# The first row block of a layer norm, DFT and MLP kernel: rows only centered, the factor of each row multiplied onto the hidden units, loads issued by two engines

## The chip, the cores and the metric

The kernel runs on one core of one Trainium2 chip. The metric is the device time of one execution in microseconds (us). Lower is better.

## The reference

For an input x of S = 2048 rows and D = 640 columns the reference computes, cut to what matters:

```python
xn = (x - mean(x)) / sqrt(var(x) + 1e-5)          # by row
a  = einsum("bsd,ed->bse", xn, dft_hid_re)
b  = einsum("bsd,ed->bse", xn, dft_hid_im)
y  = einsum("ts,bse->bte", dft_seq_re, a) - einsum("ts,bse->bte", dft_seq_im, b)
h  = gelu(einsum("bsd,df->bsf", xn, w1) + b1, approximate=True)     # F = 1536 hidden units
out = x + y + einsum("bsf,fd->bsd", h, w2) + b2
```

The change is in the first quarter of the rows of the MLP (the line of h and the last product). What matters for it: the mean is taken off a row ahead of the product with w1, and the factor 1/sqrt(var + 1e-5) is one number for each row, so that it can be multiplied in ahead of the product or behind it, as long as it is ahead of b1 and gelu.

## The kernel before

**Numbers.** TensorE multiplies operands of a type called fp32r. Every fp32 operand is split into a high part (a copy of type fp32r) and a low part (the rest), and a product is three matmuls: high by high, high by low, low by high. `split` (L154 to L161) does this: ScalarE (ACT) copies the high part at L160, VectorE (DVE) subtracts at L161. So each operand costs one instruction on ACT and then one on DVE.

**Tiling.** The MLP works with rows as the free axis of its products: the 2048 rows are cut in 4 blocks of 512, the 640 columns in ND = 5 tiles of 128, the 1536 hidden units in NF = 12 groups of 128, called units here. For a block of rows, `hidden(g)` (L289 to L304) makes unit g: 5 column tiles by 3 matmuls = 15 products of 128x512, summed in PSUM bank g % 3. `gelu(g)` (L310 to L320) takes the bank: gelu with the bias b1 on ACT (L314, into the tile `ab`), the high part on ACT (L318), the low part on DVE (L320), both into `hs`. `output(g)` (L322 to L333, with `product` at L277 to L279) makes 15 products with w2 into banks 3 to 7, where the five output tiles of a block stay until its 12 units are through. `outs` then clears the banks: bias on ACT (L344), transpose on DVE (L347), addition to x on GpSimd (POOL, L349). Block 0 is units g = 0 to 11, block 1 is g = 12 to 23. Behind these two blocks come the DFT and the rest of the MLP, which the change does not touch.

**The order.** The schedule is manual: each engine executes its instructions in the order in which the program writes them and waits where an operand isn't there yet. DMAs are issued by SyncE (SP) nearly everywhere, in written order too. So the order of calls is the order in each queue.

**The start.** `load_x` (L178) loads the first 512 rows as four chunks of 128 rows, all issued on SP. While they travel, 19 warm-up matmuls on zeros (L648) keep TensorE (PE) at work; they read tiles that share buffers with the raw w1 tiles, so the loads of w1 (L255) wait until the warm-up is through with these. For each chunk DVE takes mean and variance (`ln_stats`, L185 and L186; for chunk 1 ACT does it by two sums, L672 to L678), then `ln_scale` (L192 to L197) makes the factor: a root on ACT, a reciprocal and one Newton step on DVE. The rows are centered and multiplied (chunks 0 and 1 on ACT, L686; chunks 2 and 3 on DVE, L208), PE transposes them (`transpose_x`, L667) into banks 3 to 7, and `split` brings the five banks to SBUF as `xtt`, the operand of the units. The first piece of w1 is split at L706 and L711. Then come `hidden(0)` and `hidden(1)`, with the preparation of w1 and w2 for the next units between.

**The loop over units.** From there a loop runs over g. For each unit i of block 0 it writes, in this order:

```python
prep_w1(i + 3); prep_w2(i + 1)      # splits of w1 and w2: ACT, DVE
load_w1(i + 6); load_w2(i + 4)      # SP
first_block(i)
acc = hidden(g + 2)                 # PE
gelu(g + 2, acc)                    # ACT, ACT, DVE
output(g)                           # PE
```

`first_block(i)` (L886 to L912) prepares the later blocks beside this. At i = 0 and 1 the normed rows 0 to 3 (chunks) are made again and stored to a DRAM tile `xs`. At i = 2 to 5 DVE takes the statistics of chunks 4 to 7. At i = 6 their factor and scaling (L201) follow, then 16 stores to `xs` (L203) and four loads of `z`, which brings block 1's rows back in the order in which DVE can transpose them. At i = 8 and 9 DVE does the first two transposes of z (`transpose_z`, L238) and the statistics of chunks 8 to 11. In the iteration i = 9 the five splits of block 1's `xtt` stand between `hidden(11)` and `gelu(11)`. At i = 10 chunks 8 to 11 are scaled and stored, and at i = 11 the matrices of the hidden DFT begin to be loaded (`wraw`) and are transposed on DVE (L372) and split in the units of block 1. The last two iterations of block 0 have another order on PE: output(10), hidden(12), hidden(13), output(11).

Of the kernel before, what the change touches and what calls it, by code (L numbers as in the profile page):

```python
# [15 lines left out]
P = 128  # L16
Q = 4
B = 32
EPS = 1e-5
NWARM = 19  # L20
NGATE = (7, 10)
TAIL = 4
PADL = 8


@with_exitstack
def kernel(
# [78 lines left out]
    def bank(k):  # L106
        return banks[:, k]
# [68 lines left out]
    def load_x(c, eng=nc.sync):  # L176
        xt[c] = row_tile(f"x{c}")
        eng.dma_start(xt[c], x[c * P : (c + 1) * P])  # L178

    def ln_stats(c):  # L180
        m = MV
        st = ST[c % 2]
        half = D // 2
        for h in range(2):
            nc.vector.bn_stats(st[:, h, :], xt[c][:, h * half : (h + 1) * half])  # L185
        nc.vector.bn_aggr(m[:, c % 4, 0:2], st.rearrange("p a b -> p (a b)"))  # L186

    def ln_scale(c0, n):

        m = MV[:, c0 % 4 : c0 % 4 + n]  # L190
        ve, r, t = m[:, :, 2], m[:, :, 3], m[:, :, 4]
        nc.scalar.activation(r, m[:, :, 1], AF.Sqrt, bias=eps[:, 0:1])  # L192
        nc.vector.tensor_scalar(ve, m[:, :, 1], EPS, None, op0=ALU.add)
# [11 lines left out]
    def ln_apply_chunked(dst, c, j0=0, j1=ND):  # L205

        m = MV[:, c % 4]
        nc.vector.tensor_scalar(  # L208
            chunked(dst)[:, :, j0:j1],
            xt[c].rearrange("p (q c i) -> p q c i", q=Q, i=B)[:, :, j0:j1],  # L210
            m[:, 0:1],
            m[:, 3:4],
            op0=ALU.subtract,
            op1=ALU.mult,
        )
# [29 lines left out]

    W1, W2, w1r, w2r = {}, {}, {}, {}

    def load_w1(i, eng=nc.sync):
# [5 lines left out]
        for q in range(Q):  # L254
            eng.dma_start(t[q * B : (q + 1) * B], v[q, :, :, i * P : (i + 1) * P])  # L255

    def load_w2(i, eng=nc.sync):
        if i >= NF:
# [27 lines left out]
    def unit(g):  # L286
        return g if g < NF else LATE[g % NF]

    def hidden(g):  # L289
        i = unit(g)  # L290
        acc = bank(g % 3)
        kinds = ((0, 0), (0, 1), (1, 0))
        steps = [(j, k) for j in range(ND) for k in range(3)]
        if g == 0:
            steps = FIRST
        if g == 1:

            steps.sort(key=lambda s: s[1] == 2)
        for n, (j, k) in enumerate(steps):
            a, b = kinds[k]  # L300
            nc.tensor.matmul(  # L301
                acc, W1[i][:, a, j * P : (j + 1) * P], XT[j][:, b], start=n == 0, stop=n == len(steps) - 1
            )
        return acc  # L304
# [5 lines left out]
    def gelu(g, acc, fill=lambda k: None):  # L310

        i = unit(g)
        a = AB[:, g % 2]
        nc.scalar.activation(a, acc, AF.Gelu_apprx_tanh, bias=b1c[:, i : i + 1])  # L314
        fill(0)
        hs = HS[:, g % 3]
        HT[g] = hs
        nc.scalar.activation(hs[:, 0], a, AF.Copy)  # L318
        fill(1)
        nc.vector.tensor_tensor(hs[:, 1], a, hs[:, 0].bitcast(F32), op=ALU.subtract)  # L320

    def output(g):  # L322
        t, i = divmod(g, NF)
        if i == 0:
            oacc[t] = [bank(3 + e) for e in range(ND)]
        second(t, i, unit(g), HT[g])
# [301 lines left out]

    zeros = rows.tile([P, TB], F32, tag="yt", bufs=2, name="zeros")

    warms = [early.tile([P, TB], F32R, tag="w1r", bufs=3, name=f"warm{k}") for k in range(3)]
# [6 lines left out]
    for warm in warms:  # L638
        nc.vector.tensor_copy(warm, zeros)

    nc.scalar.activation(eps[:, 1:2], eps[:, 0:1], AF.Sqrt)
    load_w1(0)
    load_w1(1)

    wacc = bank(0)
    for k in range(NWARM):
        warm = warms[sum(k >= n for n in NGATE)]
        nc.tensor.matmul(wacc, warm[:, :P], warm, start=True, stop=True)  # L648
    load_w1(2)
    load_w2(0)  # L650
# [1 line left out]
    load_w2(1)  # L652
    load_w2(2)

    for tag, size, keys in PLACES:
        t = whole[tag] = place(tag, (P, size // 4))
        for k, key in enumerate(keys):
            slots[key] = t[:, k * 2 * D : (k + 1) * 2 * D].rearrange("p (a b) -> p a b", a=2)
    for j in range(ND):
        new_xt(0, j)  # L660
    tacc = [bank(3 + j) for j in range(ND)]
# [5 lines left out]
            nc.tensor.transpose(tacc[j][:, c * P : (c + 1) * P], xp[:, c, j * P : (j + 1) * P], ident)  # L667


    m = MV[:, 1]  # L670
    scratch = AB.rearrange("p a b -> p (a b)")
    nc.scalar.activation(scratch[:, :D], xt[1], AF.Copy, accum_out=m[:, 4:5])  # L672
    ln_stats(0)
    ln_scale(0, 1)
    nc.scalar.activation(m[:, 5:6], m[:, 4:5], AF.Copy, scale=-1.0 / D)
    nc.scalar.activation(scratch[:, :D], xt[1], AF.Square, bias=m[:, 5:6], accum_out=m[:, 2:3])
    nc.scalar.activation(m[:, 1:2], m[:, 2:3], AF.Copy, scale=1.0 / D)
    nc.scalar.activation(m[:, 0:1], m[:, 5:6], AF.Copy, scale=-1.0)  # L678

    def center(c):  # L680
        n = MV[:, c]
        nc.vector.scalar_tensor_tensor(n[:, 5:6], n[:, 0:1], -1.0, n[:, 3:4], op0=ALU.mult, op1=ALU.mult)

    def apply_on_act(c, j0, j1):
        n = MV[:, c]
        nc.scalar.activation(  # L686
            chunked(xp[:, c])[:, :, j0:j1],
            xt[c].rearrange("p (q c i) -> p q c i", q=Q, i=B)[:, :, j0:j1],
            AF.Identity,
            bias=n[:, 5:6],  # L690
            scale=n[:, 3:4],
        )

    center(0)
    apply_on_act(0, 0, ND)
    for c in (2, 3):
        ln_stats(c)
    transpose_x(0, 0, ND)
    ln_scale(1, 3)
    center(1)  # L700

    W1[0], first_w1 = slots[1, 0], w1r.pop(0).rearrange("p a b -> p (a b)")
    for j0, j1 in ((0, 2), (2, ND)):
        apply_on_act(1, j0, j1)
        if j0 == 0:
            nc.scalar.activation(W1[0][:, 0], first_w1, AF.Copy)  # L706
        for c in (2, 3, 1):
            if c != 1:
                ln_apply_chunked(xp[:, c], c, j0, j1)
            transpose_x(c, j0, j1)  # L710
    nc.vector.tensor_tensor(W1[0][:, 1], first_w1, W1[0][:, 0].bitcast(F32), op=ALU.subtract)  # L711
# [6 lines left out]
    acc0 = hidden(0)  # L718
    prep_w1(1)
    acc1 = hidden(1)  # L720
    prep_w2(0)
    prep_w1(2)
    load_w2(3)
    load_w1(5)

# [277 lines left out]
    for g in range(NG):  # L1003
        t, i = divmod(g, NF)
        if t == 0:
            prep_w1(i + 3)
            prep_w2(i + 1)
            load_w1(i + 6)
            load_w2(i + 4)
            first_block(i)  # L1010
            if i == NF - 1:
                open_w()
                acc = hidden(g + 2)
                output(g)

                def fill(k):
                    for e in ((0,), (1, 2))[k]:
                        add_block(xo[0], e, oacc[0][e], f"ot0_{e}", bias=b2c[:, e : e + 1])

                gelu(g + 2, acc, fill)  # L1020
                outs(0, (3, 4))
            elif i == NF - 2:
                output(g)
                gelu(g + 2, hidden(g + 2))
            else:
                acc = hidden(g + 2)
# [703 lines left out]
```

## Time and profile before

| | us |
|---|---|
| three runs before | 853.48, 853.95, 853.95 |
| their median | 853.95 |
| the profiled execution, its own time | 853.7 |
| its span on the core | 851.9 |
| PE busy | 842.7 (99%) |
| DVE busy | 661.1 (78%) |
| ACT busy | 353.6 (42%) |
| POOL busy | 48.1 (6%) |
| mean clock granted to TensorE | 0.998 |

In the rows of the timeline the first number is the start from the beginning of the span, the second the time that the group covers, both in us; then come the engine, the source line, the operation, what it writes and reads, the shapes, the count, and in brackets the idle time ahead of the group with what ended it. SPq is SyncE's queue of DMA issues. The time of a group of matmuls ends with the last one's drain, so that one matmul of 128x512 alone reads 0.39 us, though in a row of them one follows another every 0.23. Durations of rows that follow each other on one engine overlap a little for the same reason.

### The profile page before, as it was taken

The numbers are of one execution on the slowest core, as the hardware profiler recorded it, in microseconds if no ns is written. First come the engines' busy times: TensorE is split into PE (matmuls) and PEld (weight loads), VectorE is DVE, ScalarE is ACT, GpSimd is POOL, SyncE is SP. The second block draws the span as 40 slices with busy tenths as digits, with TensorE's granted clock in tenths as the row PEclk, the third lists the DMA queues.
The fourth block names the chain that finished last, engine by engine and source line by source line (L and its number), as shares of the span: only waits on it lengthen the run. The fifth ranks groups of instructions, "written<-read, shape, count | busy, mean of one in ns | idle before, by whom it ended". The sixth has DMA issues, their size and how long they took to land.

```text
span 851.9 us, 10326 instructions
## 1 busy us (share of the span) xinstructions
PE 842.7 (99%) x3711; PEld 695.8 (82%) x3711; DVE 661.1 (78%) x836; ACT 353.6 (42%) x496; POOL 48.1 (6%) x69
## 2 busy tenths in 40 slices
PE   8999999999999999999999999999999999999997
PEld 6888888878888888888888888888888888888885
DVE  7554766785758888879979787889967998885686
ACT  7443634456666554343444343232323423222241
POOL 0000211031211300000000000000000000000001
PEclk9999999999999999999999999999999999999999
DMA  7757698937669998958744679663865779704464
GB/s 186 215 143 199 142 228 233 225 81 190 206 223 349 360 208 161 185 110 200 160 137 105 168 215 293 159 145 97 208 169 169 252 191 228 303 19 179 125 179 99
DMA packets 207235, 158.45 MB, mean 186 GB/s; under 512 B 80848, under 2 KB 180688, under 8 KB 206672
## 3 DMA queue, kind: packets, MB, share of 16 engines
q1 hardware_dynamic: 198880, 136.03, 62.6%
q0 software_dynamic: 4080, 20.97, 6.2%
q10 hardware_dynamic: 4224, 0.79, 0.4%
q8 instruction: 29, 0.48, 0.2%
q14 instruction: 22, 0.18, 0.1%
HBM read 114.76 MB, written 42.99 MB: 185 GB/s over the span
## 4 chain that ended last, share of the span: by engine, by line
PE 98%; DVE 1%; DMA 0%; ACT 0%; issue 0%; SPq 0%; ACTq 0%
PE banks L277 29%; PE banks L279 29%; PE banks L278 29%; PE banks L301 10%; DMA x<-in_A_x_dram 0%; PE banks L667 0%; DVE st L185 0%; ACT ab L672 0%; DVE yo L1695 0%; ACT mv L192 0%; DVE mv L186 0%; DVE xp L208 0%; SPq L178 0%; DVE mv L194 0%; DVE mv L196 0%
## 5 line engine op out<-in xcount | busy, mean ns | idle before, releaser
L277 PE MATMUL banks<-as,xab 128*128 128x512 f32 x411 | 159.9, 389 | 0.0
L279 PE MATMUL banks<-as,xab 128*128 128x512 f32 x411 | 159.9, 389 | 0.0
L278 PE MATMUL banks<-as,xab 128*128 128x512 f32 x411 | 159.9, 389 | 0.0
L160 ACT ACTIVATE as<-r 128x1024 fp32r<-128x1024 f32 x80 | 85.0, 1062 | 177.0 <-PE banks L279 149.2
L161 DVE TENSOR_TENSOR as<-r,as 128x1024 fp32r<-128x1024 f32 x80 | 97.2, 1216 | 41.7 <-ACT as L160 41.6
L278 PEld LDWEIGHTS banks<-as,xab 128*128 128x128 f32 x411 | 77.1, 188 | 16.1
L277 PEld LDWEIGHTS banks<-as,xab 128*128 128x128 f32 x411 | 77.1, 188 | 16.1
L279 PEld LDWEIGHTS banks<-as,xab 128*128 128x128 f32 x411 | 77.1, 188 | 16.0
L277 PE MATMUL banks<-as,xc 128*128 128x512 f32 x224 | 87.1, 389 | 0.0
L278 PE MATMUL banks<-as,xc 128*128 128x512 f32 x224 | 87.1, 389 | 0.0
L279 PE MATMUL banks<-as,xc 128*128 128x512 f32 x224 | 87.1, 389 | 0.0
L160 ACT ACTIVATE as<-rt 128x1024 fp32r<-128x1024 f32 x32 | 34.0, 1063 | 70.8 <-PE banks L279 62.8
L301 PE MATMUL banks<-xtt,xab 128*128 128x512 f32 x240 | 56.9, 390 | 0.0
L301 PEld LDWEIGHTS banks<-xtt,xab 128*128 128x128 f32 x240 | 45.0, 188 | 9.7 <-ACT xtt L160 0.5
L278 PEld LDWEIGHTS banks<-as,xc 128*128 128x128 f32 x224 | 42.0, 188 | 8.8
L279 PEld LDWEIGHTS banks<-as,xc 128*128 128x128 f32 x224 | 42.0, 188 | 8.8
L277 PEld LDWEIGHTS banks<-as,xc 128*128 128x128 f32 x224 | 42.0, 188 | 8.7
L161 DVE TENSOR_TENSOR as<-rt,as 128x1024 fp32r<-128x1024 f32 x32 | 38.8, 1212 | 5.3 <-ACT as L160 5.3
L320 DVE TENSOR_TENSOR hs<-ab,hs 128x512 fp32r<-128x512 f32 x24 | 17.6, 733 | 32.2 <-ACT hs L318 32.2
L160 ACT ACTIVATE as<-u 128x1024 fp32r<-128x1024 f32 (+1 forms) x24 | 22.1, 919 | 48.2 <-PE banks L279 48.2
L488 DVE STREAM_TRANSPOSE r<-raw 128x1024 f32<-128x1024 f32 x32 | 39.5, 1240 | 2.3 <-PE banks L279 1.8
L488 DVE STREAM_TRANSPOSE rt<-raw 128x1024 f32<-128x1024 f32 x32 | 38.8, 1230 | 0.9 <-PE banks L279 0.8
(336 smaller groups left out, 1618.2 us busy)
## 6 DMA issues: line engine op xcount, KB each, us to landing
raw<-in_A_dft_seq_re_dram SPq DMA_DIRECT2D x64, 256.0 KB, 5.8
raw<-in_A_dft_seq_im_dram SPq DMA_DIRECT2D x64, 256.0 KB, 5.1
ws<-wit SPq DMA_DIRECT2D x15, 384.0 KB, 4.1
x<-in_A_x_dram SPq DMA_DIRECT2D x16, 320.0 KB, 4.1
xs<-x SPq DMA_DIRECT2D x64, 80.0 KB, 1.8
xo<-in_A_x_dram SPq DMA_DIRECT2D x16, 320.0 KB, 6.4
xab<-wit SPq DMA_DIRECT2D x13, 384.0 KB, 4.3
wit<-wstp POOLq DMA_DIRECT2D x12, 384.0 KB, 3.9
```

What stands on the lines that cost most here:

```text
L160: nc.scalar.activation(h, s, AF.Copy)
L161: nc.vector.tensor_tensor(l, s, h.bitcast(F32), op=ALU.subtract)
L277: nc.tensor.matmul(acc, wh, mh, start=first, stop=False, skip_group_check=goes_on)
L278: nc.tensor.matmul(acc, wh, ml, start=False, stop=False, skip_group_check=goes_on)
L279: nc.tensor.matmul(acc, wl, mh, start=False, stop=last, skip_group_check=goes_on)
L301: nc.tensor.matmul(acc, W1[i][:, a, j * P : (j + 1) * P], XT[j][:, b], start=n == 0, stop=n == len(steps) - 1)
L320: nc.vector.tensor_tensor(hs[:, 1], a, hs[:, 0].bitcast(F32), op=ALU.subtract)
L488: nc.vector.transpose(held(pieces[g][2], u).rearrange("p c (n i) -> p c n i", i=B), r.rearrange("p n (c i) -> p c n i", i=B))
```

## The change

The factor of a row is taken off the way to the first product and put behind it, for block 0 alone.

- **Loads.** Chunks 1 and 3 of x are issued by ACT, chunks 0 and 2 by SP. The warm-up is 12 matmuls on a tile that shares no buffer with w1, so the loads of w1 wait for nothing. The first piece of w1 is loaded in two parts (two and three column tiles), each by four issues.
- **Rows.** The rows of block 0 are only centered: DVE takes the mean off for chunks 0 and 2, ACT sums and centers chunk 1, and for chunk 3 ACT sums and DVE centers in two pieces. No root and no factor stand ahead of the transposes. The high and low parts of W1[0] are made in two pieces, the second between two splits of `xtt`.
- **Factor.** Behind the splits ACT takes the squares of chunks 1 and 3, the factor of all four chunks is made at once, ACT loads the table of gelu, and spreads the factors over 128 columns each. PE transposes these four tiles into bank 7, inside unit 2, behind its first ASIDE = 4 products. DVE copies bank 7 to `RB`, where each of the 128 partitions holds the 512 factors of the block.
- **Units.** For each unit of block 0 DVE multiplies the bank by RB into the tile `ab`, and gelu reads that instead of the bank. `hidden(2)` now stands ahead of the loop.
- **First output.** Output 0 does the ten products with the high part of the hidden unit first, then the five with its low part.

```diff
-NWARM = 19
-NGATE = (7, 10)
+NWARM = 12
+ASIDE = 4
...
-    def hidden(g):
+    def hidden(g, aside=None):
...
         for n, (j, k) in enumerate(steps):
+            if aside and n == ASIDE:
+                aside()
...
         a = AB[:, g % 2]
+        if g < NF:
+            nc.vector.tensor_tensor(a, acc, RB, op=ALU.mult)
+            acc = a
         nc.scalar.activation(a, acc, AF.Gelu_apprx_tanh, bias=b1c[:, i : i + 1])
...
     for c in range(NC):
-        load_x(c)
+        load_x(c, nc.scalar if c % 2 else nc.sync)
...
-    load_w1(0)
+    load_w1(0, cuts=(0, 2, ND))
...
-    (statistics, ln_scale and scaling of the four chunks: L671 to L700)
+    def sum_on_act(c):
+        nc.scalar.activation(scratch, xt[c], AF.Copy, scale=-1.0 / D, accum_out=MV[:, c, 5:6])
+
+    def square_on_act(c):
+        nc.scalar.activation(scratch, xp[:, c], AF.Square, scale=D**-0.5, accum_out=MV[:, c, 1:2])
...
+    sum_on_act(1)
+    nc.scalar.activation(
+        chunked(xp[:, 1]), xt[1].rearrange("p (q c i) -> p q c i", q=Q, i=B), AF.Identity, bias=MV[:, 1, 5:6]
+    )
+    ln_stats(0)
+    center(0, ALU.subtract, MV[:, 0, 0:1])
+    ln_stats(2)
+    center(2, ALU.subtract, MV[:, 2, 0:1])
+    sum_on_act(3)
+    center(3, ALU.add, MV[:, 3, 5:6], 0, 2)
+    center(3, ALU.add, MV[:, 3, 5:6], 2, ND)
+    first_hi(0, 2)
+    first_lo(0, 2)
     transpose_x(0, 0, ND)
+    transpose_x(1, 0, ND)
     for j0, j1 in ((0, 2), (2, ND)):
+        transpose_x(2, j0, j1)
+        transpose_x(3, j0, j1)
     for j in range(ND):
         split(XT[j][:, 0], XT[j][:, 1], tacc[j])
+        if j == 1:
+            first_hi(2, ND)
+            first_lo(2, ND)
...
     acc0 = hidden(0)
     prep_w1(1)
     acc1 = hidden(1)
+    nc.gpsimd.tensor_scalar(MV[:, 1::2, 0], MV[:, 1::2, 5], -1.0, None, op0=ALU.mult)
+    square_on_act(1)
+    square_on_act(3)
+    (high part of W1[2] on ACT)
+    ln_scale(0, NC)
+    nc.scalar.activation(eps[:, 1:2], eps[:, 0:1], AF.Gelu_apprx_tanh)
+    (low part of W1[2] on DVE)
+    wide = AB[:, 1]
+    nc.scalar.activation(
+        wide.rearrange("p (c n) -> p c n", c=NC), MV[:, :, 3:4].broadcast_to([P, NC, P]), AF.Copy
+    )
+    def spread():
+        for c in range(NC):
+            nc.tensor.transpose(bank(7)[:, c * P : (c + 1) * P], wide[:, c * P : (c + 1) * P], ident)
+    acc2 = hidden(2, spread)
     prep_w2(0)
-    prep_w1(2)
+    nc.vector.tensor_copy(RB, bank(7))
```

The lines in brackets stand for code that is told in the list above; `center(c, op, shift, j0, j1)` is one DVE instruction that adds or subtracts the mean for column tiles j0 to j1 - 1.

More of the change, by code (lines that the diff above doesn't have):

```diff
@@ L320, in gelu, with first_output @@
         nc.vector.tensor_tensor(hs[:, 1], a, hs[:, 0].bitcast(F32), op=ALU.subtract)
+    def first_output(hs):
+        w = W2[0]
+        for k in range(2):
+            for e in range(ND):
+                cols = slice(e * P, (e + 1) * P)
+                if k == 0:
+                    nc.tensor.matmul(oacc[0][e], w[:, 0, cols], hs[:, 0], start=True, stop=False)
+                    nc.tensor.matmul(oacc[0][e], w[:, 1, cols], hs[:, 0], start=False, stop=False)
+                else:
+                    nc.tensor.matmul(
+                        oacc[0][e], w[:, 0, cols], hs[:, 1], start=False, stop=False, skip_group_check=True
+                    )
     def output(g):
@@ L325, in output @@
             oacc[t] = [bank(3 + e) for e in range(ND)]
-        second(t, i, unit(g), HT[g])
+        if g == 0:
+            first_output(HT[g])
+        else:
+            second(t, i, unit(g), HT[g])
     def second(t, i, u, hs, es=range(ND)):
@@ L629 @@
     zeros = rows.tile([P, TB], F32, tag="yt", bufs=2, name="zeros")
-    warms = [early.tile([P, TB], F32R, tag="w1r", bufs=3, name=f"warm{k}") for k in range(3)]
+    RB = rows.tile([P, TB], F32, tag="yt", bufs=2, name="rb")
     for c in range(NC):
-        load_x(c)
+        load_x(c, nc.scalar if c % 2 else nc.sync)
+    for tag, size, keys in PLACES:
+        t = whole[tag] = place(tag, (P, size // 4))
+        for k, key in enumerate(keys):
+            slots[key] = t[:, k * 2 * D : (k + 1) * 2 * D].rearrange("p (a b) -> p a b", a=2)
     nc.gpsimd.memset(eps, EPS)
@@ L637 @@
     nc.vector.memset(zeros, 0.0)
-    for warm in warms:
-        nc.vector.tensor_copy(warm, zeros)
+    warm = whole["as"][:, :TB]
+    nc.vector.tensor_copy(warm, zeros)
     nc.scalar.activation(eps[:, 1:2], eps[:, 0:1], AF.Sqrt)
-    load_w1(0)
+    load_w1(0, cuts=(0, 2, ND))
     load_w1(1)
@@ L653 @@
     load_w2(2)
[L655 to L658, printed above, removed]
     for j in range(ND):
@@ new lines, in first_hi, with first_lo @@
+    def first_hi(j0, j1):
+        nc.scalar.activation(W1[0][:, 0, j0 * P : j1 * P], first_w1[:, j0 * P : j1 * P], AF.Copy)
+    def first_lo(j0, j1):
+        h, l = (W1[0][:, k, j0 * P : j1 * P] for k in range(2))
+        nc.vector.tensor_tensor(l, first_w1[:, j0 * P : j1 * P], h.bitcast(F32), op=ALU.subtract)
+    sum_on_act(1)
[4 more added lines that the diff above has]
+    center(0, ALU.subtract, MV[:, 0, 0:1])
@@ L1025 @@
             else:
-                acc = hidden(g + 2)
+                acc = hidden(g + 2) if g else acc2
                 if i == NF - 3:
```

53 lines of the change are left out of this document (16 added, 37 removed).

## The prediction

> **What bounds the kernel now.** I read the page first: its span and the chain that ended last.
>
> ```profile
> span 851.9 us, 10326 instructions
> PE 98%; DVE 1%; DMA 0%; ACT 0%; issue 0%; SPq 0%; ACTq 0%
> ```
>
> TensorE (PE) is that chain for 98% of the span, so a change ahead of its first product is worth what it moves that product, less what PE waits later. The second view is the timeline of the start, with two later rows of PE. (Hidden unit g: 15 products at L301. Its output: 15 at L277 to L279.)
>
> ```profile
> 0.74 1.83 SPq L178 DMA_DIRECT2D x<-in_A_x_dram  x4
> 1.92 6.51 PE L648 MATMUL banks<-warm 128*128 128x512 f32 x19 [1.92 <-DVE warm L639]
> 3.77 0.89 DVE L185 BATCH_NORM_STATS2 st<-x 128x6 f32<-128x320 f32 x2 [1.23 <-DMA x<-in_A_x_dram]
> 4.51 0.74 ACT L672 ACTIVATE ab<-x 128x640 f32<-128x640 f32 x1 [2.28 <-DMA x<-in_A_x_dram]
> 4.69 0.21 DVE L186 BATCH_NORM_AGGREGATE mv<-st 128x2 f32<-128x12 f32 x1
> 4.93 0.15 DVE L193 TENSOR_SCALAR mv<-mv 128x1 f32<-128x1 f32 x1
> 8.27 0.71 PE L667 MATMUL banks<-ident,xp 128*128 128x128 f32 x5
> 9.85 1.51 DVE L208 TENSOR_SCALAR xp<-x,mv 128x256 f32<-128x256 f32 x4
> 10.32 2.08 PE L667 MATMUL banks<-ident,xp 128*128 128x128 f32 x15 [1.34 <-DVE xp L208]
> 11.70 2.52 ACT L160 ACTIVATE xtt<-banks 128x512 fp32r<-128x512 f32 x5
> 12.31 3.08 DVE L161 TENSOR_TENSOR xtt<-banks,xtt 128x512 fp32r<-128x512 f32 x5 [0.21 <-ACT xtt L160]
> 12.33 10.76 PE L301 MATMUL banks<-xtt,xab 128*128 128x512 f32 x45
> 14.09 0.76 ACT L160 ACTIVATE xab<-w1r 128x640 fp32r<-128x640 f32 x1
> 15.31 0.82 DVE L161 TENSOR_TENSOR xab<-w1r,xab 128x640 fp32r<-128x640 f32 x1
> 16.12 1.28 ACT L314 ACT_TABLE_LOAD   x1
> 17.41 0.69 ACT L314 ACTIVATE ab<-banks,b1c 128x512 f32<-128x512 f32 x1
> 18.13 0.63 ACT L318 ACTIVATE hs<-ab 128x512 fp32r<-128x512 f32 x1
> 18.80 0.69 DVE L320 TENSOR_TENSOR hs<-ab,hs 128x512 fp32r<-128x512 f32 x1 [1.20 <-ACT hs L318]
> ...
> 29.73 0.39 PE L277 MATMUL banks<-hs,rt 128*128 128x512 f32 x1
> ...
> 90.93 6.96 PE L301 MATMUL banks<-xtt,xab 128*128 128x512 f32 x30
> ```
>
> The reader is to see three things. PE's first product waits to 12.33 us, behind statistics, scaling, transposes (L667) and the first split (ACT, 11.70). From there PE runs through: 30 products in 6.96 us are 0.227 each, a unit is 3.40, and the second output begins at 29.73, which is 18.03 after the first split. And the time to unit 0's output held slack that the new code uses up.
>
> **The change, part 1: the first product.** I count from S, the start of the first split (now 11.70).
>
> Loads: chunks 0 and 1 are now issued at once instead of 0.46 apart (1.83 for four). Chunk 0 landed before 3.77, chunk 1 before 4.51; if two transfers share the DMA engines both land near the later time, if not, nothing moves. I take 4.28 for the first statistics, bounds 3.77 and 4.55.
>
> DVE then does statistics 0 (3.77 to 4.69, result usable at 4.93: 1.16), centering 0 (640 columns; the four pieces of L208 hold 1280 in 1.51, so 0.52 until the next starts), statistics and centering of chunk 2 (1.68), and the first 256 columns of chunk 3 (about 0.41, a quarter of 1.51 and its drain). Root, reciprocal and Newton steps are gone from this path. With 0.43 for hand-over and transpose, S = 4.28 + 1.16 + 0.52 + 1.68 + 0.41 + 0.43 = 8.48; bounds 8.0 and 8.75. ACT's part (sum 1 and centering 1, sum 3) takes some 0.9 each from 4.5, done near 7.2, under DVE's. PE's twelve warm-up products end by 7.1 even if each is a slow one: 19 took 6.51, which is 4.3 at 0.227, so about ten ran at double. Its 10 transposes (0.11 each: five in 0.71 with the last's drain) are done before chunk 2 is.
>
> **Part 2: units 0 to 2.** A row of a later root, of the same shape as the one that the change puts on ACT here:
>
> ```profile
> 94.48 0.30 ACT L192 ACTIVATE mv<-mv,eps 128x4 f32<-128x4 f32 x1
> ```
>
> First product at S + 0.63 (11.70 to 12.33). Unit 0 waits about 0.6 inside (0.2 before: 45 products take 10.2 of the 10.76 less a drain): ACT now does the other three fifths of W1[0] (0.45 of the 0.76 at 14.09) between splits 1 and 2, DVE likewise. Unit 1 ends at S + 8.05. ACT behind the splits: W1[1] 0.76, two Squares 0.74 each (L672), W1[2] 0.76, root 0.30, table 1.28, then the factors spread over 512 columns 0.63: ready at S + 8.1, when PE asks for them at S + 8.96 (four products into unit 2). So the added work on ACT is hidden; without that cover each us of it would be one of PE.
>
> The table load ends 0.01 before the next ACTIVATE at 17.41. The Trainium skill ("ScalarE: Activation LUTs", What ACT_TABLE_LOAD costs) adds a drain and says 2.66 us for a switch; by it the factors would come at S + 9.5 and PE would wait 0.5. The trace shows no such drain, and I keep 1.28.
>
> The four spreading transposes (0.11 each) end, with drain, at S + 9.65, unit 2 at S + 11.95. Now a chain that nothing covers: copy from PSUM 0.60 (as a split on DVE, 3.08 for five), multiplication 0.69 (as L320), gelu 0.69, high part 0.63, with hand-overs 12.4. PE waits 0.45. Unit 1's multiplication stands in DVE's queue behind unit 0's low part (0.69), so W1[3]'s low part (0.82) comes at S + 16.6, and unit 3 waits 0.38 for it. The second output begins at S + 11.95 + 0.45 + 0.38 + two units of 3.4 = S + 19.58 instead of S + 18.03. Part 1 and 2 together: 8.48 + 19.58 - 29.73 = **-1.67 us** on PE.
>
> **Part 3: what is late next.** Each unit of block 0 now has a multiplication on DVE ahead of its gelu, and DVE takes its queue in order. Where that queue waits for a load, gelu waits too, which it did not before.
>
> ```profile
> 62.23 2.18 DVE L201 TENSOR_SCALAR x<-x,mv 128x640 f32<-128x640 f32 x4
> 62.87 7.33 SPq L203 DMA_DIRECT2D xs<-x  x16
> 79.96 0.71 DVE L238 STREAM_TRANSPOSE zt<-z 128x512 f32<-128x512 f32 x1 [5.65 <-DMA z<-xs]
> 82.62 0.65 DVE L320 TENSOR_TENSOR hs<-ab,hs 128x512 fp32r<-128x512 f32 x1
> 90.50 0.65 DVE L161 TENSOR_TENSOR xtt<-zt,xtt 128x512 fp32r<-128x512 f32 x1
> 91.33 0.69 DVE L161 TENSOR_TENSOR xtt<-zt,xtt 128x512 fp32r<-128x512 f32 x1 [0.19 <-ACT xtt L160]
> 91.21 0.67 ACT L314 ACTIVATE ab<-banks,b1c 128x512 f32<-128x512 f32 x1
> 95.64 2.18 DVE L201 TENSOR_SCALAR x<-x,mv 128x640 f32<-128x640 f32 x4
> 104.43 0.72 DVE L347 STREAM_TRANSPOSE ot<-banks 128x512 f32<-128x512 f32 x1 [0.56 <-POOL xo L349]
> 107.25 0.39 PE L277 MATMUL banks<-hs,xc 128*128 128x512 f32 x1
> 112.86 0.85 DVE L372 STREAM_TRANSPOSE wt<-wraw 128x640 f32<-128x640 f32 x1 [3.37 <-DMA wraw<-in_A_dft_hid_re_dram]
> 156.12 0.69 DVE L320 TENSOR_TENSOR hs<-ab,hs 128x512 fp32r<-128x512 f32 x1 [0.81 <-ACT hs L318]
> 159.16 0.39 PE L278 MATMUL banks<-hs,r 128*128 128x512 f32 x1
> 176.60 1.29 DVE L161 TENSOR_TENSOR xtt<-zs,xtt 128x512 fp32r<-128x512 f32 x2 [0.35 <-ACT xtt L160]
> 182.68 2.51 DVE L347 STREAM_TRANSPOSE zs<-banks 128x512 f32<-128x512 f32 x4 [1.28 <-ACT banks L344]
> 186.43 0.50 PE L277 MATMUL banks<-r,tw 128*128 128x512 f32 x1
> ```
>
> Three delays go into one chain. (a) Unit 7's multiplication, 0.73 with hand-over, delays the scaling at 62.23, so the 16 stores on SP, so z, for which DVE waits until 79.96. (b) Behind z and two statistics stood unit 10's low part (82.62), its gelu long done; now DVE must multiply there, then wait for gelu and high part: 0.69 + 0.69 + 0.63 and hand-overs, 2.15. (c) Unit 11's gelu stood on ACT at 91.21; now it waits for DVE to finish block 1's last split and multiply: 1.45.
>
> Block 1's splits are thus late by 0.73 + 2.15 = 2.88 against PE. Product 14 of unit 12 (90.93 + 13 x 0.227 = 93.88) needs the one that ended at 92.02: margin 1.86, so PE waits 1.0, and stands at -0.65. Behind (c) the chain is late by -1.67 + 0.73 + 2.15 + 1.45 = +2.7 on the clock. The last bank is cleared 105.15 and used 107.25, margin 2.1; that chain is about 2.2 late (unit 13's gelu had 0.5 to spare): 2.2 + 0.65 - 2.1 = 0.75 more, PE at +0.1. The scaling at 95.64 is late by 2.7, and SP's stores, loads and the weights at 112.86 behind it, in order; unit 20's low part ends 156.81 for 159.16, margin 2.35: PE at +0.35. At 176.60 and 182.68 DVE was idle for 0.35 and 1.28, which it regains: 2.7 - 1.63 = +1.05, and at 186.43 PE waits for DVE already. **Sum: -1.67 + 1.0 + 0.75 + 0.25 + 0.7 = +1.0 us.** The profiled execution took 853.7 us, inside the runs (853.48 to 853.95): **854.7 us**. The tail behind PE stays.
>
> **The rivals.** *The gain stands*: were z or the weights earlier than the order on SP says, or the chain given more idle time than I found, PE keeps most of -1.67: 852.0, and with only the first wait (1.0) 853.0. For it: DVE is idle 5.65 ahead of 79.96. Against: that idle time is the wait for z itself, and cannot be used.
>
> *The lateness is not regained* (slower): DVE finds neither the 0.35 nor the 1.28, because ACT's part ahead of them is late too, and the full 2.7 reaches PE at 186: 853.7 + 2.7 = 856.4. It decides from 0.7 more than I count.
>
> *The clock stays low* (slower): with 12 warm-up products instead of 19, PE's rate may not be at its full one when unit 0 starts; 15 products more at twice 0.227 cost 3.4, so 858. Against: in the profile only transposes stand between the last warm-up product and 12.33, nearly 4 us, and 45 products then ran at full rate; the new stretch is shorter, some 2.4. The Trainium skill ("TensorE: Matmul & The Clock Gate", Parts 1 and 4) says that about 3.4 us of sustained work release the clock and that transposes do not count as work; by that rule this rival is live, by the trace it is not.
>
> *The loads win nothing*: chunk 0 later than 4.55, or W1's first pieces, now issued behind chunk 2, slowing chunk 3: S past 9.2, everything 0.75 later, 855.4.
>
> **How the numbers follow.** A difference under 0.2% (1.7 us) is about what a measurement of this kernel can tell from none. Forecast 0.60 (853.2 to 855.6 by the bounds of S and 0.5 either way on the margins); gain stands 0.16, half of it over 0.2%; not regained 0.14; clock 0.04; loads 0.06. Faster by over 0.2%: 0.10. Slower: 0.14 + 0.04 and a part of the loads' case, 0.20. Same: 0.70. The range, 852.3 to 856.7, leaves out some of the first rival and of the clock's.
>
> **What would show it.** Right: the first product of unit 0 near 9.1; PE idle near 0.45 ahead of output 0; unit 10's multiplication behind z's first transpose; PE waits in unit 12 near 91 to 94 and for the last bank near 107. Wrong: unit 12 running through in 3.40, the scaling of chunks 8 to 11 starting before 97, or a first product after 9.8.

## The result, and the profile after

The changed kernel takes 856.81 us (median of 7 runs, 856.10 to 858.28) against 853.95 (7 runs, 853.48 to 854.48): 1.0034 times the time before, 95% interval 1.0025 to 1.0043. It is slower by 2.9 us. The forecast was 854.7 with a range to 856.7, so the measured time lies outside it. The profiled execution took 856.63 us, with a span of 854.8.

First the page of the changed kernel, its span and the chain that ended last:

```profile
span 854.8 us, 10321 instructions
PE 81%; DMA 5%; DVE 5%; issue 3%; SPq 3%; ACT 2%; POOL 0%; DVEq 0%; ACTq 0%; POOLq 0%
```

Before, PE was that chain for 98% of the span. Now 19% of it runs over other engines and DMAs. Next what PE waited for, in the view of waits (total, times, longest, in us):

```profile
PE banks L673 <- DVE as L665: 1.9, 1, 1.9
PE banks L278 <- ACT banks L856: 1.0, 1, 1.0
PE banks L304 <- DVE xtt L161: 0.7, 2, 0.4
PE banks L334 <- ACT hs L324: 0.4, 1, 0.4
PE banks L278 <- DVE ot L369: 0.2, 1, 0.2
```

The first wait is the start and was there before. The other four are new: the first output (L334), block 1's splits in unit 12 (L304), the last bank of block 0 (L369), and at 183 us a bank that ACT updates (L856). (The view counts the idle time behind the modelled end of a product. By the starts of the products PE loses more at such a place, as the table below shows.) The line numbers have moved: L304 is the hidden product, L318, L320, L324 and L326 are multiplication, gelu, high part and low part. The timeline of the changed kernel, with the rows that answer to those of the prediction:

```profile
1.90 5.49 PE L673 MATMUL banks<-as 128*128 128x512 f32 x12 [1.90 <-DVE as L665]
4.55 0.89 DVE L185 BATCH_NORM_STATS2 st<-x 128x6 f32<-128x320 f32 x2 [2.71 <-DMA x<-in_A_x_dram]
7.19 2.77 PE L688 MATMUL banks<-ident,xp 128*128 128x128 f32 x20
9.23 1.08 ACT L160 ACTIVATE xtt<-banks 128x512 fp32r<-128x512 f32 x2 [1.75 <-PE banks L688]
9.88 8.66 PE L304 MATMUL banks<-xtt,xab 128*128 128x512 f32 x34
21.91 0.51 PE L334 MATMUL banks<-hs,rt 128*128 128x512 f32 x1 [0.39 <-ACT hs L324]
29.27 0.39 PE L278 MATMUL banks<-hs,rt 128*128 128x512 f32 x1
62.51 2.18 DVE L201 TENSOR_SCALAR x<-x,mv 128x640 f32<-128x640 f32 x4
80.64 0.71 DVE L238 STREAM_TRANSPOSE zt<-z 128x512 f32<-128x512 f32 x1 [6.04 <-DMA z<-xs]
83.31 0.64 DVE L318 TENSOR_TENSOR ab<-banks,rb 128x512 f32<-128x512 f32 x1
85.40 0.69 DVE L326 TENSOR_TENSOR hs<-ab,hs 128x512 fp32r<-128x512 f32 x1 [1.46 <-ACT hs L324]
94.18 0.69 DVE L161 TENSOR_TENSOR xtt<-zt,xtt 128x512 fp32r<-128x512 f32 x1 [0.18 <-ACT xtt L160]
94.79 0.68 DVE L318 TENSOR_TENSOR ab<-banks,rb 128x512 f32<-128x512 f32 x1
96.93 0.69 DVE L326 TENSOR_TENSOR hs<-ab,hs 128x512 fp32r<-128x512 f32 x1 [1.46 <-ACT hs L324]
160.60 1.25 DVE L785 STREAM_TRANSPOSE zt<-z 128x1024 f32<-128x1024 f32 x1
183.52 0.71 DVE L369 STREAM_TRANSPOSE ab<-banks 128x512 f32<-128x512 f32 x1
184.32 0.58 ACT L856 ACTIVATE banks<-banks 128x512 f32<-128x512 f32 x1 [2.64 <-DVE ab L369]
185.50 2.51 DVE L369 STREAM_TRANSPOSE zs<-banks 128x512 f32<-128x512 f32 x4 [1.28 <-ACT banks L366]
```

Two rows of the kernel before, unit 11's low part and the transpose that closes block 1, to lay beside 96.93 and 183.52:

```profile
92.57 0.69 DVE L320 TENSOR_TENSOR hs<-ab,hs 128x512 fp32r<-128x512 f32 x1 [0.55 <-ACT hs L318]
180.69 0.71 DVE L347 STREAM_TRANSPOSE ab<-banks 128x512 f32<-128x512 f32 x1
```

Read it in three steps. The first product is 2.45 us earlier (9.88 for 12.33), and the second output still 0.46 (29.27 for 29.73). Then unit 10's multiplication stands behind z's transpose and two statistics (83.31), and its low part 1.46 behind that with DVE idle. And the row that closes block 1 on DVE, the transpose at 183.52, is 2.83 later than the same one in the kernel before, at 180.69; the whole execution is longer by about as much (2.9).

From unit 3 on the products on PE are the same in both kernels, so each can be laid beside its counterpart, counted from the end. The difference of their starts is PE's lateness (below zero: a lead), in us. S is the start of the first split; the last column is the same DVE transpose against 180.69. Each line is one profiled execution. The runs of one kernel spread by 1.1 (e8) to 3.4 us (e5), so a few tenths between two lines say little.

| kernel | S | at 30 | at 100 | at 112 | at 190 | at the end | DVE transpose |
|---|---|---|---|---|---|---|---|
| changed | 9.23 | -0.46 | 1.19 | 1.76 | 2.83 | 2.79 | 2.83 |
| e1_no_mult | 8.60 | -2.19 | -2.19 | -2.19 | -2.19 | -2.15 | -2.19 |
| e2_no_mult_10_11 | 8.87 | -0.81 | -0.81 | -0.81 | -0.79 | -0.34 | -0.81 |
| e3_unit10_first | 9.26 | -0.44 | -0.44 | -0.44 | 0.96 | 0.88 | 0.94 |
| e4_warm9 | 8.51 | -1.12 | 0.45 | 1.03 | 2.71 | 2.68 | 2.71 |
| e5_x_sp | 9.25 | -0.43 | 1.16 | 1.73 | 4.07 | 4.34 | 4.08 |
| e6_pool_mult | 8.56 | -1.10 | 0.93 | 1.98 | 3.41 | 3.50 | 3.39 |
| e7_stats_late | 8.59 | -1.04 | -1.04 | -1.04 | -1.04 | -1.12 | -1.04 |
| e8_z_early | 9.26 | -0.41 | -0.42 | -0.41 | -0.41 | -0.33 | -0.42 |
| e9_aside1_z_early | 8.83 | -1.20 | -1.20 | -1.20 | -1.20 | -1.22 | -1.21 |
| e10_aside1 | 8.56 | -1.50 | 0.14 | 0.72 | 2.77 | 2.72 | 2.76 |

Where the last two columns on PE differ (e2, e5), PE loses the rest in short waits near 207 and 673 us, whose cause was not followed.

### The profile page after: what moved, and what is told of

Read it like the earlier page. It is cut to its first block, busy times and chain, and to the rows that moved or that the text cites. A ratio compares the mean times of both kernels' runs of the same rounds, so it can differ in the third digit from the quotient of the medians.

```text
span 854.8 us, 10321 instructions
## 1 busy us (share of the span) xinstructions
PE 844.4 (99%) x3708; PEld 695.4 (81%) x3708; DVE 667.1 (78%) x838; ACT 354.1 (41%) x497; POOL 48.8 (6%) x70
## 4 chain that ended last, share of the span: by engine, by line
PE 81%; DMA 5%; DVE 5%; issue 3%; SPq 3%; ACT 2%; POOL 0%; DVEq 0%; ACTq 0%; POOLq 0%
PE banks L278 26%; PE banks L279 26%; PE banks L280 26%; DMA wit<-wst 2%; PE banks L304 2%; SPq L386 1%; DMA z<-xs 1%; SPq L256 1%; DMA w2r<-in_B_w_dram 1%; SPq L203 1%; DMA x<-in_A_x_dram 1%; DVE xtt L161 0%; DVE x L201 0%; ACT ab L320 0%; DVE zt L238 0%
## 5 line engine op out<-in xcount | busy, mean ns | idle before, releaser
L304 PE MATMUL banks<-xtt,xab 128*128 128x512 f32 x240 | 58.9, 395 | 0.8 <-DVE xtt L161 0.7
L304 PEld LDWEIGHTS banks<-xtt,xab 128*128 128x128 f32 x240 | 44.4, 188 | 12.6 <-DVE xtt L161 2.2
L161 DVE TENSOR_TENSOR as<-u,as 128x1024 fp32r<-128x1024 f32 (+1 forms) x24 | 24.9, 1042 | 18.8 <-ACT as L160 18.8
```

The source lines that it names most:

```text
L161: nc.vector.tensor_tensor(l, s, h.bitcast(F32), op=ALU.subtract)
L304: nc.tensor.matmul(acc, W1[i][:, a, j * P : (j + 1) * P], XT[j][:, b], start=n == 0, stop=n == len(steps) - 1)
```

## The experiments

Theory A: the multiplications of units 7, 10 and 11 stand in DVE's queue at places where it waits for a load or for splits, and this makes the chain behind block 1's rows late, which sets the time at 183 us. Rival B: the loads, which the change put on other queues, are what is late. Rival C: it is 8.3 us more work on DVE as such.

### Without the multiplications

```diff
-        if g < NF:
+        if g < 0:                # e1_no_mult
+        if g < NF - 2:           # e2_no_mult_10_11
             nc.vector.tensor_tensor(a, acc, RB, op=ALU.mult)
```

> Leaves out the multiplication of the units by the factors (RB is still made, nothing reads it), so the output lacks the factors in block 0. Theory A (the multiplications of units 7, 10 and 11 stand in DVE's queue where it waits for a load or for splits, and this makes the later chains late): PE's lead over the kernel before, 0.6 us at unit 3, stays through unit 12, the clearing of the last bank and the stretch at 182 us; and the 0.5 us ahead of output 0 is partly gone too: 852.7 to 853.3 us. Rival B (the loads: the change moved loads on the queues, and z and the weights of the hidden DFT come late for that reason): the waits in unit 12, near 108 us and near 183 us stay, 856 us or more. Rival C (8.3 us more work on DVE as such): like A here.

> Leaves out the multiplication for units 10 and 11 alone, 2 of 12, so these two units lack the factors. Theory A: the two delays of 2.15 and 1.45 us are gone, DVE's chain is late only by what z is late (0.7), of which 0.35 is regained before 182 us: PE has no wait in unit 12 or at the last bank, and the profiled execution takes some 854.0 us (853.4 to 854.4). Rival C (work on DVE as such, 2 of 12 parts of it gone): 856.1 us. Rival B (loads): 856.6.

Measured: e1_no_mult 852.07 us (ratio 0.9977, 0.9967 to 0.9986), e2_no_mult_10_11 853.67 (0.9991, 0.9982 to 1.0001). Without any multiplication PE keeps all of its lead to the end, so rival B falls as the main cause: the loads were on the changed queues here too. A small part is left of it. In all eleven kernels with the change, e1 among them, z comes 0.34 to 0.49 later behind the scaling at 62 us than before; why is open. e1 came out 0.6 below its range: PE had no wait for the first output at all, and its S was 8.60, not 9.23. With ten of the twelve multiplications kept, nearly all of the lateness is gone. Rival C said 856.1 for that, and falls as well. The only waits of PE in e2 are the start and the first output:

```profile
PE banks L673 <- DVE as L665: 1.9, 1, 1.9
PE banks L334 <- ACT hs L324: 0.4, 1, 0.4
```

### Unit 10 multiplied before z arrives

```diff
-            first_block(i)
+            if i != 8:
+                first_block(i)
...
                 gelu(g + 2, acc)
+                if i == 8:
+                    first_block(i)
                 output(g)
```

> All multiplications are done; only the DVE work of first_block(8) (the first transpose of z and two statistics) is written behind gelu(10) instead of ahead of hidden(10), so that unit 10 is multiplied while z is still on its way. Theory A: the 2.15 us of unit 10 are gone and its multiplication costs nothing; splits of block 1 come 2.1 us earlier, PE waits nothing in unit 12 and little at the last bank; DVE's chain is late by some 1.1 at 163 us and 0.75 at 183: 854.4 us (853.8 to 855.0). Rival C: no change, 856.6. Rival B: z is as late as before, the waits stay, 856.6.

Measured: 854.12 us (1.0002, 0.9992 to 1.0011), inside the expected range. On DVE, in e3's timeline:

```profile
77.09 0.69 DVE L318 TENSOR_TENSOR ab<-banks,rb 128x512 f32<-128x512 f32 x1 [2.46 <-PE banks L304]
79.24 0.69 DVE L326 TENSOR_TENSOR hs<-ab,hs 128x512 fp32r<-128x512 f32 x1 [1.45 <-ACT hs L324]
80.64 0.71 DVE L238 STREAM_TRANSPOSE zt<-z 128x512 f32<-128x512 f32 x1 [0.71 <-DMA z<-xs]
94.19 0.69 DVE L326 TENSOR_TENSOR hs<-ab,hs 128x512 fp32r<-128x512 f32 x1 [1.45 <-ACT hs L324]
```

The multiplication, its wait of 1.45 and the low part all fit into the time in which DVE waited for z before. z comes at 80.64 as in the changed kernel, and unit 11's low part at 94.19 instead of 96.93. PE waits neither in unit 12 nor at the last bank; what is left is the wait at 183 us, by 0.94 of DVE.

### The start by itself: fewer warm-up products, another queue, an earlier spread

```diff
-NWARM = 12
+NWARM = 9                        # e4_warm9
-        load_x(c, nc.scalar if c % 2 else nc.sync)
+        load_x(c)                # e5_x_sp
-ASIDE = 4
+ASIDE = 1                        # e10_aside1
```

> Nine warm-up matmuls instead of twelve. In the profile of the change the twelve all ran at 0.43 us each and held PE until 7.19, the transposes of chunk 0 (ready at 6.28) ran at 0.21 each, and the rate doubled only at 8.05 (in the kernel before at 6.04). If the rate doubles by the time since the first matmul whatever runs, transposes begin at 6.3, the first split comes at 8.8 to 9.0 instead of 9.23, and the time is 0.2 to 0.4 us shorter at unit 3. If transposes do not count as work for the clock, the rate stays at half through the transposes and some of unit 0's products: the first split at 9.4 or later and up to 3.4 us lost in units 0 and 1.

> All four chunks of x issued by SP as in the kernel before, the rest as changed. Chunk 0 then lands near 3.7 us instead of 4.5 and DVE's centering ends some 0.7 earlier, but PE is held by the warm-up until 6.6 to 7.2 and by 20 transposes behind it. Theory A (PE's warm-up and its clock set the first split; the later lateness comes from DVE's queue): first split between 8.6 (clock up early) and 9.3 (late), and the time stays at 856.3 to 857.0. Rival B (the two queues are what wins at the start): first split 0.5 or more later than 9.23, the time 857 or more.

> The changed kernel with ASIDE = 1 and nothing else. Theory A: the same 0.6 us is gained at unit 3, and given back in unit 12, at the last bank and at 183 us, because there DVE's chain sets the time: 856.6 us as before (856.1 to 857.2). If a gain at the start counted, 856.0 or less.

Measured: 856.57 us (1.0029, 1.0018 to 1.0040), 857.89 (1.0042, 1.0028 to 1.0055) and 856.45 (1.0032, 1.0020 to 1.0043). In e4 the first split came at 8.51, earlier than the 8.8 to 9.0 of its first case; the late one of its second case, 9.4 or more, did not occur. e4 and e10 answer the main question. At 30 us their lead is 1.12 and 1.50 instead of 0.46, and at 190 us they stand where the changed kernel stands: 2.71 and 2.77 late. All that the start gained more came back as waits, as e10's view of PE's waits shows:

```profile
PE banks L278 <- ACT banks L856: 2.0, 1, 2.0
PE banks L673 <- DVE as L665: 1.9, 1, 1.9
PE banks L304 <- DVE xtt L161: 0.7, 2, 0.4
PE banks L278 <- DVE ot L369: 0.2, 1, 0.2
```

The wait at the bank that ACT updates is 2.0 instead of 1.0, the other two are as they were. The next table follows the chain on DVE: how much later than in the kernel before (first column, us) each of its rows starts.

| row, its start before | changed | e3 | e4 | e5 | e6 | e10 |
|---|---|---|---|---|---|---|
| scaling of chunks 4 to 7, 62.23 | 0.28 | 0.30 | -0.38 | 0.31 | 0.92 | -0.75 |
| first transpose of z, 79.96 | 0.68 | 0.68 | -0.02 | 0.67 | 1.35 | -0.34 |
| last split of block 1, 91.33 | 2.85 | 0.11 | 2.12 | 2.81 | 2.60 | 1.80 |
| scaling of chunks 8 to 11, 95.64 | 4.36 | 1.62 | 3.64 | 4.31 | 4.66 | 3.31 |
| transpose of a later z, 157.33 | 3.27 | 1.27 | 3.14 | 4.52 | 3.83 | 3.20 |
| transpose that closes block 1, 180.69 | 2.83 | 0.94 | 2.71 | 4.08 | 3.39 | 2.76 |

Up to the scaling of chunks 8 to 11 the chain inherits the whole of what the start gained: e4 and e10 are 0.72 and 1.05 ahead of the changed kernel there. Then come stores, loads and weights, and at the next row both stand within 0.13 of it. DVE was still 1.9 us ahead in e10 at 138 us, and then waited for rows of a later block from SP, in e10's timeline:

```profile
160.53 1.25 DVE L785 STREAM_TRANSPOSE zt<-z 128x1024 f32<-128x1024 f32 x1 [4.38 <-DMA z<-xs]
```

SP had lost the lead before that. It issued the stores of the first output 1.10 earlier than in the changed kernel (116.94 for 118.04), but the loads of z behind them, for which it waits until DMAs have landed, at about the same time. First the changed kernel, then e10:

```profile
126.49 1.91 SPq L234 DMA_DIRECT2D z<-xs  x4
126.38 2.01 SPq L234 DMA_DIRECT2D z<-xs  x4
```

SP's queue goes on from there, and the loads for which DVE waits near 160 start at 151.17 in e10 and 150.82 in the changed kernel. So the chain behind the splits is one of DMAs too, and in these two profiles 0.7 or 1.0 us at the start did not move it. Why the DMAs took longer there is open. The stretch from the scaling at 95.64 to the row at 157.33 takes 60.2 to 61.9 us in the twelve profiles, so it can take or give about 1 us. The times of e4 and e10 are 0.24 and 0.36 below the changed kernel's, with intervals that overlap, and a gain of that size is not excluded.

In e5, with all chunks on SP, chunks 2 and 3 are late. DVE waits 1.27 for chunk 2, and ACT's row for the sum of chunk 3 stands at 7.62, against 6.32 in the changed kernel. SP issues the four chunks in 1.82 us, one after another; whether the pieces of w1 that travel beside them slow them as well is not shown.

```profile
7.62 0.74 ACT L694 ACTIVATE ab<-x 128x640 f32<-128x640 f32 x1 [1.40 <-DMA x<-in_A_x_dram]
```

S was 9.25 although the clock doubled early, at 5.45, where kernels with both queues and an early clock had 8.51 to 8.60. So the two queues are worth some 0.7 us of S in that case. What they are worth in time e5 does not show: its lead at 30 us, 0.43, is that of the changed kernel, whose clock doubled late. Theory A had expected 857.0 at most here, rival B 857 or more with a later S; the time, from four runs between 855.71 and 859.12, is above A's range. In the profile the chain is as late as in the changed kernel up to the scaling of chunks 8 to 11 (4.31 for 4.36). The 1.25 that it is later at the end (4.08 for 2.83) arise at a store on POOL's queue for which DVE waited 4.21 us near 159, in the changed kernel 2.84. Why it was later is open.

### The multiplication on GpSimd

```diff
-            nc.vector.tensor_tensor(a, acc, RB, op=ALU.mult)
+            if g < 3:
+                nc.vector.tensor_tensor(a, acc, RB, op=ALU.mult)
+            else:
+                nc.scalar.activation(a, acc, AF.Copy)
+                nc.gpsimd.tensor_tensor(a, a, RB, op=ALU.mult)
```

> For units 3 to 11 ACT copies the bank to the tile ab and GpSimd multiplies it there by the factors, instead of DVE from the bank; units 0 to 2 as changed. More work in all (0.6 on ACT and 1.3 on GpSimd for 0.69 on DVE), but none of it in DVE's queue. Theory A: units 7 and 10 delay nothing any more; unit 11's low part waits some 2 us on DVE for copy, GpSimd, gelu and high part, which stays in the chain: PE late by 1.0 to 1.5 at 183 us, 854.6 to 855.3 us. Rival C (work as such): also faster, but then no wait for unit 11 is seen in DVE's rows. If latency of each unit is what costs, slower than 856.6.

Measured: 856.35 us (1.0027, 1.0016 to 1.0038), 1.0 above the expected range; the profiled execution, 857.54, is one of the slowest of six that go from 854.72 to 857.57. Unit 10 no longer holds DVE, as expected. But unit 7 does delay the chain. The scaling of chunks 4 to 7 is 0.92 late although PE's lead was 1.10, since its root stands on ACT behind a wait of 1.40 for GpSimd. z comes 0.67 later than in the changed kernel, and unit 11 holds the queues longer, in e6's timeline:

```profile
81.31 0.71 DVE L238 STREAM_TRANSPOSE zt<-z 128x512 f32<-128x512 f32 x1 [6.07 <-DMA z<-xs]
84.18 0.89 DVE L185 BATCH_NORM_STATS2 st<-x 128x6 f32<-128x320 f32 x2 [1.15 <-DMA x<-in_A_x_dram]
95.81 0.72 ACT L324 ACTIVATE ab<-ab,b1c 128x512 f32<-128x512 f32 x1 [1.42 <-POOL ab L322]
97.23 0.69 DVE L330 TENSOR_TENSOR hs<-ab,hs 128x512 fp32r<-128x512 f32 x1 [2.61 <-ACT hs L328]
```

ACT now waits for GpSimd in each unit (1.42 in unit 11), with the splits of w1 and w2 behind it, and DVE waits for ACT. The waiting has moved to another queue in order and grown. This fits a price that is the length of the path from bank to low part, wherever the multiplication is done, at the places where something is queued behind it.

### The order put right

In e7_stats_late the two edits are e3's and this one, which puts work into DVE's idle 1.45 us of unit 11:

```diff
             transpose_z(1, i - 8)
-            ln_stats(2 * i - 8)
-            ln_stats(2 * i - 7)
+            if i == 8:
+                ln_stats(8)
+                ln_stats(9)
...
-                gelu(g + 2, acc)
+                gelu(g + 2, acc, (lambda k: ln_stats(10 + k)) if i == NF - 3 else (lambda k: None))
```

e8_z_early has this edit, leaves `first_block(8)` where it was, and writes `first_block(6)` one unit earlier:

```diff
-            first_block(i)
+            if i != 6:
+                first_block(i)
...
+                if i == 5:
+                    first_block(6)
                 gelu(g + 2, acc, ...)
```

e9_aside1_z_early is e8 with ASIDE = 1.

> As e3_unit10_first (DVE work of first_block(8) behind gelu(10)), and the statistics of chunks 10 and 11 moved from ahead of block 1's splits into the wait of DVE between unit 11's multiplication and its low part. Theory A: this fills the 1.45 us idle there; DVE's chain at 183 us goes from 0.94 late to some 0.5 early, so PE keeps the lead of the start: 853.1 us by the profile (852.6 to 853.7), depending on when the clock doubled at the start. If something else ties the chain at 183 us, it stays at 854.1 or more.

> The changed order of the units stays, but first_block(6) (factors and scaling of chunks 4 to 7, their stores, the loads of z and of chunks 8 to 11) is written one unit earlier, between hidden(7) and gelu(7); the statistics of chunks 10 and 11 stand in unit 11's gap as in e7_stats_late. Theory A: z comes 5 us or more earlier, DVE no longer waits for it ahead of unit 10's multiplication, the splits of block 1 and all behind them are early, and PE keeps the lead of the start: 852.6 to 853.4 us. If DVE's work as such binds, 856 us; if gelu(7) behind the table loads is late for output 7, PE waits near 63 us and the lead is smaller.

> e8_z_early with the four spreading transposes behind one product of unit 2 instead of four (ASIDE = 1). In the trace of e8_z_early PE reaches the transposes 0.9 us after the factors are spread on ACT, waits 0.4 for output 0 and 0.3 for unit 3. Theory A: RB and the first multiplication come 0.68 earlier, both waits go, and since nothing later binds PE keeps it: 0.6 us less than e8_z_early, 852.3 us (851.7 to 852.9). If the first output is tied to something else (the table, the high part), no change from 852.9.

Measured: 852.93 us (0.9989, 0.9980 to 0.9998), 852.91 (0.9988, 0.9979 to 0.9997) and 852.63 (0.9986, 0.9977 to 0.9995). All three are faster than the kernel before, if by 0.1% only, with all twelve multiplications in. In e7's timeline the gap of unit 11 is full:

```profile
89.39 0.68 DVE L318 TENSOR_TENSOR ab<-banks,rb 128x512 f32<-128x512 f32 x1
89.99 0.88 DVE L185 BATCH_NORM_STATS2 st<-x 128x6 f32<-128x320 f32 x2
92.02 0.64 DVE L326 TENSOR_TENSOR hs<-ab,hs 128x512 fp32r<-128x512 f32 x1
```

And in e8's timeline the scaling that z depends on, and z itself, come 6 us earlier than at 62.51 and 80.64:

```profile
56.49 2.18 DVE L201 TENSOR_SCALAR x<-x,mv 128x640 f32<-128x640 f32 x4
74.57 0.70 DVE L238 STREAM_TRANSPOSE zt<-z 128x512 f32<-128x512 f32 x1
```

In e9 PE waits for nothing behind its first instruction, in the view of its waits:

```profile
PE banks L673 <- DVE as L665: 1.9, 1, 1.9
```

e10 and e9 are the same edit of the start, once with the late chain and once without. The times do not tell the two cases apart (856.45 for 856.81, and 852.63 for e8's 852.91: in both pairs the intervals overlap, and e9's gain of 0.3 is half of the expected 0.6). The profiles do: in e10 a lead of 1.50 at 30 us ends as 2.72 late, in e9 one of 1.20 ends as 1.22.

## Why the prediction was wrong, step by step

**Part 1, S = 8.48: 9.23.** Rows 4.55, and the first split waiting 1.75 for PE, show what failed. The statistics began at the bound (4.55 for 4.28). The last piece of the transposes, not DVE, came last: the twelve warm-up products ended near 7.1 as bounded, but I priced the transposes behind them at 0.11 each, the price of a clock that has doubled. Here 20 took 2.77, and the first four ran at 0.21. With the clock up early S was 8.51 to 8.60 (e1, e4, e6, e7, e10), close to the forecast.

**Part 2, second output at S + 19.58: 29.27, or S + 20.04.** The waits were where they were put, ahead of output 0 and in unit 3: PE's row 21.91 shows 0.39 of wait for the high part, against 0.45. The lead was 0.46 instead of 1.67: 0.75 of the shortfall is S, 0.46 the rest. The rest is mainly unit 0, which waited 0.78 inside instead of 0.6 (before it had waited 0.38, where the forecast read 0.2), the copy, 0.69 for 0.60, and output 0, whose 15 products took 3.57 for 3.40. The added work on ACT was hidden, as forecast: the table load took 1.28 and the factors were spread at S + 8.02, forecast S + 8.1.

**Part 3, delays (b) and (c).** Both have the predicted size. From z's transpose to the last split the changed kernel takes 94.87 - 80.64 = 14.23, before 92.02 - 79.96 = 12.06: 2.17 more, predicted 2.15. Unit 11's low part is 4.36 late on the clock (96.93 for 92.57 before) and the split 2.85, so (c) was 1.51, predicted 1.45.

**Part 3, the lateness of the chain on the clock.** This is the term of the sum that was mis-sized most. I subtracted the whole lead of PE, 1.67, and came to +2.7. Measured is +4.36, which is 0.68 + 2.17 + 1.51. The first term replaces -1.67 + 0.73 = -0.94: the scaling came at 62.51, 0.28 late and not early, since PE's lead was 0.46 and not 1.67, and z added 0.40 by itself on its way through SP and DMA. That is 1.62 of the difference: 1.21 of lead and 0.40 of z.

The missing lead alone does not explain the miss, though. e10 had most of it, 1.50. Its chain was 3.31 late at the scaling of chunks 8 to 11, and the next step of the forecast would have left 3.31 - 1.63 = 1.68 behind the transpose at 183 us. Measured is 2.76 at the transpose, and PE is 2.77 late at 190.

**Part 3, what DVE regains.** This is the step that failed by its mechanism. The sum regained the idle 0.35 at 176.60 and the idle 1.28 at 182.68, and let the chain meet PE behind both, at 186.43. The first came true: behind the transpose of z near 160 the chain regains 0.33 to 0.44 in each kernel of the second table. The second did not, since PE meets the chain ahead of it. Two rows of the kernel before, then the one of the changed kernel:

```profile
181.49 0.58 ACT L810 ACTIVATE banks<-banks 128x512 f32<-128x512 f32 x1 [2.39 <-DVE ab L347]
182.13 0.50 PE L277 MATMUL banks<-xtt,tw 128*128 128x512 f32 x1
184.95 0.50 PE L278 MATMUL banks<-xtt,tw 128*128 128x512 f32 x1 [0.96 <-ACT banks L856]
```

In the kernel before, ACT updated a bank behind DVE's transpose of 180.69, and PE's next product began 0.06 after the end of that (182.07). There was no margin: what the transpose is late, PE is late, 2.83 and 2.82 here. The idle 1.28 lies behind that point. Nor is it a reserve for what follows, for it is still there in all six kernels, ahead of 185.50 in the changed one: ACT ends it, and ACT starts (184.32) behind DVE's own transpose of 183.52.

The changed kernel regained 4.36 - 2.83 = 1.53 all the same, but 1.09 of it in the stretch of stores and loads between 100 and 160 us, where the other five regained between -0.21 and 0.83. That this is near 1.63 is luck.

The rival "the lateness is not regained" (856.4, given 0.14) was right that the 1.28 is not found. That its time is near, too, is partly luck: it let 2.7 through in full, where 4.36 came in and 1.53 was regained.

**The clock rival** (858, 0.04) was right about the clock and wrong about the price. The slow products were the warm-up and the first transposes, not unit 0, and they cost 0.7 of S. A cost in time is not seen: e4 and e10, with S at 8.51 and 8.56, took as long within the intervals. **The gain stands** is what the change would have been without its multiplications (e1) or with the order put right (e9).

**The form of the sum** hid this. Its terms on PE were 1.0 in unit 12, 0.75 at the last bank, 0.25 near 159 and 0.7 at 183; PE's starts show 1.65, 0.57, nothing and 1.06. Where the chain that sets the time is on another engine, these waits only take up the lead that is left. A gain on PE shortens the time only if the chain inherits it and nothing behind gives it back. In e4 the chain inherited all of the 0.66 us more lead at 62 us (61.85 for 62.51), and 0.12 of it was left at the DVE transpose, behind the wait for z near 160.

## What to carry to other kernels

An instruction added in front of a queue in order costs not its own 0.7 us but the whole path from its operand to its result, at every place where the queue waits for something else first; look for these places (a load, a transpose of a late tile) and write the new work ahead of them. When a gain is at the start and a loss further on, follow the chain that sets the end back to where it leaves the improved engine, credit it with what it inherits there, and then look at each wait for a load or store behind it, which can take that credit away. Idle time on a late engine counts as reserve only if it lies ahead of the place where the other engine meets the chain, and if what ends it does not itself wait for the late engine.

## What the runs showed of the hardware

The clock of TensorE did not double at a fixed time after the first product. The starts of the products show it: at half rate one 128x512 product follows another every 0.43, at full rate every 0.23, and a 128x128 transpose every 0.21 or 0.11. Twelve warm-up products that started at 1.90 or 1.91 took between 4.56 and 5.49 us in different profiles. The changed kernel's row (5.49) stands above; this is the one of e6_pool_mult:

```profile
1.91 4.56 PE L677 MATMUL banks<-as 128*128 128x512 f32 x12 [1.91 <-DVE as L669]
```

All twelve at half rate give 5.49; at 0.43 slow and 0.23 fast, 0.93 less are between four and five fast ones, so the clock doubled near 5.3 in e6. In the changed kernel it doubled behind the fourth of the transposes, near 8.05. That is 3.4 and 6.1 us after the first product. S goes with it in the profiles with both queues: 8.51 to 8.60 in e1, e4, e6, e7 and e10, whose clock had doubled by 6.63 us, and 9.23 to 9.26 in the changed kernel, e3 and e8, where it doubled at 8.05 to 8.10. It is not the only thing that moves S: in e9 (8.83) the clock doubled at 6.67, but chunk 0 landed 0.28 later than in e10. The Trainium skill ("TensorE: Matmul & The Clock Gate", Part 1) says that the activity window is free-running, some 3.4 us long, so that the point of change depends on where in it the first matmul falls. The traces agree that the point changes from execution to execution, but over 2.8 us, wider than the 500 ns either way that it names; the window itself no run here shows. In the kernel before the first split came at 11.70, behind all of that; in the changed kernel the transposes ahead of it fall inside it.
